# A Linformer attention and MLP-mixer kernel: fixed program order with the next batch's front in steps, crossbar turns of q and u, packed k and v projections

## The chip, the core and the metric

One Trainium2 chip, one of its cores. TensorE multiplies matrices into PSUM (8 banks of 128 x 512 f32), VectorE and ScalarE read PSUM and write SBUF, GpSimd issues the loads that convert f32 to bf16, SyncE issues stores and crossbar turns (transposes made by the DMA engines on the way from SBUF to SBUF). The metric is the device time of one launch in microseconds (us); smaller is better. Profiles are of one execution; their span is about 1.8 us shorter than the time of that launch.

Ratios below are the mean time of one kernel's fast runs over that of the kernel before in the same rounds, so they are not quite the ratio of the medians that stand beside them.

## The reference, cut to what matters

Eight batches; 8 heads of 64; 1024 positions; k and v are projected from 1024 positions to 64 before the attention.

```python
k_proj = np.einsum('ks,bhsd->bhkd', E, k)          # E, F: 64 x 1024
v_proj = np.einsum('ks,bhsd->bhkd', F, v)
scores = q @ k_proj.T / 8;  attn = softmax(scores) # 1024 x 64 per head
x = (attn @ v_proj), heads side by side            # 1024 x 512 per batch
h = relu(x.T @ w_tok1) @ w_tok2                    # token mixing, 256 wide
u = x + h.T
out = u + relu(u @ w_ch1) @ w_ch2                  # channel mixing, 1536 wide
```

I call channel mixing the *main* part (192 matmuls of 512 columns per batch) and everything up to u the *front*.

## The kernel before

The order on each engine is left to a scheduler; `attention(b + 1)` stands before `mixer(b)` in the program. All PSUM tiles come from one pool of 8 banks. The parts that matter:

```python
def attention(b):
    # loads of k, v, q: 8 heads x 128 KB each, on GpSimd
    # q regrouped by head pairs, then turned on TensorE, 32 transposes per batch:
    for hp in range(HP):
        for sj in range(2):
            for ss in range(4):
                nc.tensor.transpose(qt_ps[...], q2_sb[:, hp, si]..., ident)
            nc.vector.tensor_copy(out=qT_sb[...], in_=qt_ps)
    for si in range(NSI):      # v projection: 8 matmuls onto 64 partitions
        nc.tensor.matmul(vproj_ps, FT_sb[:, si, :], v_sb[:, :, si, :], ...)
    ...                        # k projection the same, 8 more
    ...                        # per head pair: two score matmuls on 64 x 64 tiles, exp
    for ss in range(4):        # denominators by a matmul of their own
        nc.tensor.matmul(dn_ps[:, 2*ss : 2*ss+2], lhs, bd_ones, ...)
        nc.tensor.matmul(ou_ps[:, ss, :], lhs, vbd_sb[:, hp, :], ...)
def mixer(b, x_sb):
    ...                        # token mixing, 16 + 16 matmuls of 512 columns
    nc.tensor.transpose(ut_ps[...], u_sb[...], ident)      # 32 per batch
    ...                        # main: gT_ps (up), ReLU, g_ps (down), add u, store
xs[0] = attention(0)
# load wt1, wt2, wc1, wc2 (the last two 1.5 MB each) on the same queue
for b in range(B):
    if b + 1 < B: xs[b + 1] = attention(b + 1)
    mixer(b, xs[b])
```

The softmax here doesn't subtract the row's maximum and nothing guards it: scores larger than these inputs give would overflow.

## Time and profile before

572.56 us median of 4 runs (571.37 to 573.18). TensorE's spacing of two matmuls of 512 columns is 0.217 us, so the main part takes 41.7 us per batch.

| | us |
|---|---|
| first up matmul of batch 0 | 85.0 |
| from the up matmuls of batch 3 (279.31) to those of batch 4 (344.06) | 64.75 |
| of that, main part | 41.7 |
| of that, front | 23 |

The profile's page in 40 slices of the span: busy tenths of TensorE and the load of the DMA engines, then the chain of work that ended last, by engine.

```profile
PE   1540889999999999998999999999999999999997
...
DMA  9999992129502390028601391020001200020012
...
PE 71%; DVE 14%; DMA 6%; POOL 5%; issue 2%; ACT 1%; DVEq 0%; ACTq 0%; POOLq 0%
```

From the seventh slice to the last but one TensorE is busy for at least eight tenths of each slice (nine tenths of nearly all), and it holds 71% of the chain: it is the limit. In the first four slices (57 us) it is busy about half the time at most, while the DMA row is full for the first six.

TensorE's waits, longest in total first (in total, times, longest), and the two ends of the long one in its timeline (start, duration, instruction, in brackets the idle time just before):

```profile
PE qt_ps L109 <- ACT q_sb L99: 34.4, 5, 19.9
PE tp_ps L143 <- DVE kproj_sb L139: 8.0, 8, 1.1
```

```profile
20.81 3.65 PE L109 MATMUL qt_ps<-ident,q_sb 128*128 128x128 bf16 x32 [13.81 <-ACT q_sb L99]
...
56.05 1.03 PE L109 MATMUL qt_ps<-ident,q_sb 128*128 128x128 bf16 x8 [19.88 <-ACT q_sb L99]
...
85.04 5.15 PE L233 MATMUL gT_ps<-uT_sb,wc_sb 128*128 128x512 bf16 x22
```

Batch 1's q transposes waited 19.9 us for loads that stand behind the two large weight loads in the queue; they began at 56.05, and batch 0's main part came after all of batch 1's attention, at 85.04.

The front of one batch in the steady state, on TensorE (starts and durations of merged groups):

```profile
300.27 20.88 PE L242 MATMUL g_ps<-wc_sb,gT_sb 128*128 128x512 bf16 x96
320.99 1.95 PE L109 MATMUL qt_ps<-ident,q_sb 128*128 128x128 bf16 x32
322.87 1.91 PE L120 MATMUL vproj_ps<-v_sb,FT_sb 128*64 128x512 bf16 x8
324.62 1.89 PE L134 MATMUL kproj_ps<-k_sb,ET_sb 128*64 128x512 bf16 x8
327.49 0.29 PE L143 MATMUL tp_ps<-ident,kproj_sb 64*128 64x64 bf16 x4 [0.98 <-DVE kproj_sb L139]
...
333.99 3.61 PE L198 MATMUL h_ps<-x_sb,wt_sb 128*128 128x512 bf16 x16
...
344.06 21.12 PE L233 MATMUL gT_ps<-uT_sb,wc_sb 128*128 128x512 bf16 x96
```

Between the end of the main part (321) and the next (344.06) TensorE spends 2 us on q transposes, 3.6 on the two projections, waits 0.98 for the copy of k, spends 6 us on scores, denominators and outputs (lines left out), and the last 10 (from 333.99) on token mixing, 7, and the u transposes, 3.2 with their waits.

### The profile page before, as it was taken

The page shows a single profiled execution, that of the slowest core. Times are in us where ns is not written, and L with a number is a line of the kernel's source. Part 1 is how long each engine was busy: PE and PEld are TensorE (multiplying, and loading weights), DVE is VectorE, ACT ScalarE, POOL GpSimd, SP SyncE. Part 2 cuts the span into 40 slices and gives each one's busy share as a digit, 9 for nine tenths or more (in the row PEclk, how much of TensorE's full clock was granted, in tenths as well). Part 3 has the DMA queues.
Part 4 walks back from the last instruction along what each step waited for, and adds up shares of the span by engine and source line. Part 5 has one row for each costly group of instructions (what it writes and reads, how often), then busy time and mean ns, then how long its engine had stood idle before and what let it go on. Part 6 is the DMA issues. An engine that isn't in the chain of part 4 may idle for free.

```text
span 570.8 us, 7698 instructions
## 1 busy us (share of the span) xinstructions
PE 509.8 (89%) x3120; PEld 259.4 (45%) x3120; DVE 210.4 (37%) x524; ACT 175.9 (31%) x288; POOL 110.9 (19%) x212
## 2 busy tenths in 40 slices
PE   1540889999999999998999999999999999999997
PEld 0330454454544454445544454445544454445443
DVE  1440571137502572028602563027601563025012
ACT  0221336305260235304260235404261034500720
POOL 8608871006200360006200260000000000000000
PEclk9975889999999999999999999999999999999999
DMA  9999992129502390028601391020001200020012
GB/s 135 208 208 202 201 201 44 38 92 151 91 0 79 102 186 4 27 103 134 109 1 73 94 185 19 20 102 28 1 1 69 80 2 0 18 94 38 1 55 92
DMA packets 39555, 46.90 MB, mean 82 GB/s; under 512 B 4192, under 2 KB 30304, under 8 KB 39520
## 3 DMA queue, kind: packets, MB, share of 16 engines
q0 software_dynamic: 30304, 29.63, 32.4%
q1 hardware_dynamic: 9216, 16.78, 7.5%
q8 instruction: 24, 0.39, 0.3%
q14 instruction: 11, 0.09, 0.1%
HBM read 59.24 MB, written 16.78 MB: 133 GB/s over the span
## 4 chain that ended last, share of the span: by engine, by line
PE 71%; DVE 14%; DMA 6%; POOL 5%; issue 2%; ACT 1%; DVEq 0%; ACTq 0%; POOLq 0%
PE gT_ps L233 29%; PE g_ps L242 29%; DVE u_sb L213 6%; PE h_ps L198 5%; DMA wc_sb<-in_moe_w_ch_dram 4%; DVE qT_sb L114 2%; PE ou_ps L178 2%; PE ut_ps L219 2%; POOL v_sb L90 2%; POOL q_sb L94 2%; PE u_ps L209 2%; POOL k_sb L89 1%; DVE x_sb L183 1%; PE dn_ps L175 1%; DVE vbd_sb L128 1%
## 5 line engine op out<-in xcount | busy, mean ns | idle before, releaser
L233 PE MATMUL gT_ps<-uT_sb,wc_sb 128*128 128x512 bf16 x768 | 169.0, 379 | 0.0
L242 PE MATMUL g_ps<-wc_sb,gT_sb 128*128 128x512 bf16 x768 | 167.1, 379 | 0.0
L238 ACT ACTIVATE gT_sb<-gT_ps 128x512 bf16<-128x512 f32 x184 | 109.0, 597 | 111.6 <-PE gT_ps L233 110.5
L247 DVE TENSOR_TENSOR o_sb<-g_ps,u_sb 128x512 f32<-128x512 f32 x64 | 44.3, 692 | 267.7 <-PE g_ps L242 267.7
L242 PEld LDWEIGHTS <-gT_sb 128*128 128x128 bf16 x768 | 75.1, 98 | 90.7
L233 PEld LDWEIGHTS <-wc_sb 128*128 128x128 bf16 x768 | 74.8, 98 | 90.7 <-issue 3.8
L90 POOL DMA_DIRECT2D v_sb<-in_v_dram x64 | 34.7, 545 | 203.2 <-PE vproj_ps L120 188.5
L99 ACT COPY q_sb<-q_sb 128x1024 bf16<-128x1024 bf16 x23 | 23.1, 1044 | 133.8 <-PE qt_ps L109 109.8
L166 ACT ACTIVATE attnT_sb<-sco_ps 128x512 bf16<-128x512 f32 x64 | 33.0, 602 | 61.2 <-PE sco_ps L161 61.2
L109 PE MATMUL qt_ps<-ident,q_sb 128*128 128x128 bf16 x256 | 19.5, 242 | 34.4 <-ACT q_sb L99 34.4
L213 DVE TENSOR_TENSOR u_sb<-u_ps,x_sb 128x512 bf16<-128x512 f32 x64 | 39.0, 683 | 21.2 <-PE u_ps L209 21.2
L183 DVE TENSOR_TENSOR x_sb<-ou_ps,rdn 128x512 bf16<-128x512 f32 x64 | 41.7, 681 | 1.7
L89 POOL DMA_DIRECT2D k_sb<-in_k_dram x64 | 34.6, 554 | 14.9 <-DMA wc_sb<-in_moe_w_ch_dram 6.8
L94 POOL DMA_DIRECT2D q_sb<-in_q_dram x64 | 34.0, 534 | 10.1 <-issue 5.3
L109 PEld LDWEIGHTS <-q_sb 128*128 128x128 bf16 x256 | 17.6, 109 | 37.1 <-ACT q_sb L99 35.5
L114 DVE COPY qT_sb<-qt_ps 128x512 bf16<-128x512 bf16 x64 | 23.0, 417 | 19.2 <-PE qt_ps L109 19.1
L175 PE MATMUL dn_ps<-bd_ones,attnT_sb 128*128 128x2 bf16 x256 | 27.4, 171 | 2.8 <-ACT attnT_sb L166 1.5
L178 PE MATMUL ou_ps<-vbd_sb,attnT_sb 128*128 128x128 bf16 x256 | 29.8, 221 | 0.0
L198 PE MATMUL h_ps<-x_sb,wt_sb 128*128 128x512 bf16 x128 | 29.7, 386 | 0.0
L209 PE MATMUL u_ps<-hT_sb,wt_sb 128*128 128x512 bf16 x128 | 28.9, 379 | 0.0
L175 PEld LDWEIGHTS <-attnT_sb 128*128 128x128 bf16 x256 | 20.0, 96 | 16.2 <-ACT attnT_sb L166 10.8
L219 PE MATMUL ut_ps<-ident,u_sb 128*128 128x128 bf16 x256 | 21.5, 221 | 5.1 <-DVE u_sb L213 4.6
(46 smaller groups left out, 260.0 us busy)
## 6 DMA issues: line engine op xcount, KB each, us to landing
out_dram<-o_sb SPq DMA_DIRECT2D x64, 256.0 KB, 2.0
k_sb<-in_k_dram POOLq DMA_DIRECT2D x64, 128.0 KB, 4.9
v_sb<-in_v_dram POOLq DMA_DIRECT2D x64, 128.0 KB, 4.9
q_sb<-in_q_dram POOLq DMA_DIRECT2D x64, 128.0 KB, 4.9
wc_sb<-in_moe_w_ch_dram POOLq DMA_DIRECT2D x2, 1536.0 KB, 18.8
wt_sb<-in_moe_w_tok_dram POOLq DMA_DIRECT2D x2, 512.0 KB, 7.4
E_sb<-in_E_dram POOLq DMA_DIRECT2D x1, 128.0 KB, 3.1
F_sb<-in_F_dram POOLq DMA_DIRECT2D x1, 128.0 KB, 3.4
```

The source lines that it names most:

```text
L90: nc.gpsimd.dma_start(out=v_sb[:, h, :, :], in_=v[b, h].rearrange(rr, p=P))
L94: nc.gpsimd.dma_start(out=q_sb[:, h, :, :], in_=q[b, h].rearrange("(p si) d -> p si d", p=P))
L175: nc.tensor.matmul(dn_ps[:, 2 * ss : 2 * ss + 2], lhs, bd_ones, start=True, stop=True)
L178: nc.tensor.matmul(ou_ps[:, ss, :], lhs, vbd_sb[:, hp, :], start=True, stop=True)
L183: nc.vector.tensor_tensor(out=x_sb[:, sj * 4 : sj * 4 + 4, h0 * D : (h0 + 2) * D] .rearrange("p s (j d) -> p s j d", j=2), in0=ou_ps.rearr ...
L198: nc.tensor.matmul(h_ps, wt1_sb[:, sc, tc_i * P : (tc_i + 1) * P], x_sb[:, sc, :], start=(sc == 0), stop=(sc == SC - 1),)
L209: nc.tensor.matmul(u_ps, wt2_sb[:, tc_i, sc::NSI], hT_sb[:, tc_i, :], start=(tc_i == 0), stop=(tc_i == TC - 1),)
L213: nc.vector.tensor_add(out=u_sb[:, sc, :], in0=u_ps, in1=x_sb[:, sc, :])
L233: nc.tensor.matmul(gT_ps, wc1_sb[:, dc, cc * P : (cc + 1) * P], uT_sb[:, dc, s_lo : s_lo + S2], start=(dc == 0), stop=(dc == DMC - 1),)
L238: nc.any.tensor_relu(out=gT_sb[:, cc, s_lo : s_lo + S2], in_=gT_ps)
L242: nc.tensor.matmul(g2_ps, gT_sb[:, cc, sc * P : (sc + 1) * P], wc2_sb[:, cc, :], start=(cc == 0), stop=(cc == CC - 1),)
L247: nc.vector.tensor_add(out=o_sb, in0=g2_ps, in1=u_sb[:, sc, :])
```

## The change

Its intent: take off TensorE what others can do, and let no chain of small dependent steps of the front stop it.

1. The order on every engine is the program's (manual schedule). The front of batch b+1 is a generator of 31 steps, spread as if they were 33; after each block of 4 main matmuls of batch b, zero to two steps are issued.
2. q and u are turned through the crossbar by SyncE's DMAs (batches 1 to 7).
3. The k projection goes to partitions 0 to 63 of a bank and the v projection to 64 to 127, so the two matmuls of a pair use different column tiles of TensorE.
4. The denominator is a 65th column of v (a column of ones), so its matmuls go.
5. Batch 0 is loaded and computed by head pairs; the large weights are loaded last.
6. Main PSUM has 4 banks, the front 2, the output tile 2; 3 of 8 ReLUs go to VectorE.

The diff, cut to its core:

```diff
+    ctx.enter_context(tc.manual_schedule())
+    def turn_q(b):
+        for j in range(2):
+            nc.sync.dma_start_transpose(out=st["qT", b][:, hs]..., in_=st["q", b][:, hs]...)
+    def kv_mm(b, kv_ps, hs, sis):
+        for si in sis:
+            nc.tensor.matmul(kv_ps[0:KP, 0:n], EFT[:, si, 0:KP], st["k", b][:, hs, ds], **f)
+            nc.tensor.matmul(kv_ps[KP:P, 0:n], EFT[:, si, KP:P], st["v", b][:, hs, ds], **f)
-                    nc.tensor.matmul(
-                        dn_ps[:, 2 * ss : 2 * ss + 2], lhs, bd_ones, start=True, stop=True
-                    )
+            nc.tensor.matmul(                       # ou_step, 130 columns, 4 per head
+                ou[:, s // 2, o : o + 2 * D1], at[:, s * P : (s + 1) * P], vbd[:, h, :], ...)
+    def front(b):
+        turn_q(b)
+        yield
+        for j in range(4):
+            kv_mm(b, kv_ps, slice(0, H), range(2 * j, 2 * j + 2))
+            if j < 3:
+                yield
+        kv_vec(b, kv_ps, kprojs, slice(0, H))       # 1 ScalarE copy, 3 VectorE copies
+        if b + 1 < B:
+            load_kv(b + 1, (0, H)); load_q(b + 1, (0, H))
+        yield
+        kt_step(...)                                # k turned on TensorE
+        yield
+        ats = {0: score_step(b, 0, kT, front_ps)}
+        yield
+        for h in range(H):
+            if h + 1 < H:
+                ats[h + 1] = score_step(b, h + 1, kT, front_ps)
+            ou_step(b, h, ats.pop(h))
+            yield
+        ...                                         # token mixing, 8 + 8 steps
+            if s % 2 == 1:
+                nc.sync.dma_start_transpose(out=st["uT", b][:, s - 1 : s + 1]..., ...)
+    front_first()                                   # batch 0 by head pairs
+    for b in range(B):
+        for n, _ in enumerate(mains()):             # one block of 4 main matmuls
+            want = 0 if n < first else min(n_front, 1 + (n - first) * n_front // (last - first))
+            while done < want:
+                done += 1
+                next(fr, None)
```

`front_first` computes `attn(0)`, then `attn(hp)` and `mix(hp - 1)` in turn, then `mix(3)`.

## The prediction

> **What bounds the kernel now.** TensorE. The page gives matmuls 89% of the 570.8 us span and the chain of waits puts 71% on it. The timeline shows two regimes. (a) Start: the first channel-mixing (up) matmul begins at 85.0 us. Until then TensorE waits 34.4 us in total for the regrouped q (waits view); the DMA strip reads full for 80 us, and the two weight DMAs of 1536 KB stand in front of batch 1's loads. (b) Steady state: one batch takes 64.7 us (300.27 to 365.01). Channel mixing is 192 matmuls of 512 columns at 0.217 us = 41.7 us. The other 23 us are the front: q transposes 1.9, v and k projections 3.6, a hole of about 1.7 around the k transposes, scores 1.75, denominator/output pairs 3.75, token mixing 6.9, u transposes 3.2 with waits.
>
> **What the change does per batch, on TensorE.**
> - q and u transposes leave TensorE from batch 1 on: -5.1 us.
> - k and v projections as two 64-column tiles side by side: 16 slots become 8. Traced score pairs took 0.215 us: -1.8 us.
> - The denominator column goes into the output product (130 columns): 32 pairs become 32 matmuls of about 0.06 us (q transposes' pitch): about -1.9.
> - The holes of the front are filled by channel mixing: about -1.7.
> - Added: about 26 changes of tiling mode. The Trainium skill, "TensorEngine Tiling (Array Packing)", Key Properties, says a mode change drains the array; the trace's outputs-to-scores step costs 0.15 instead of 0.06 us, so about 0.1 each, +2.6.
> - Added waits: the output tile has one buffer, and reciprocal 0.19 plus multiply 0.68 on VectorE, queued behind ReLUs of 0.69, must finish in about 1.4 us between steps: estimate +1.5. Last u turn before the next batch's up matmuls: +0.5.
>
> Front about 16 us, so a period near 58 instead of 64.7, all on the critical path: about 7 x 6.7 = 47 us.
>
> **Start.** Batch 0 is loaded by head pairs, small weights early, large ones behind, and computed pair by pair. By the traced 0.2 MB/us, pair 1 lands near 15 us; attention plus mixing of one pair is an estimated 10.5 us chain, much of it waits. Channel mixing of batch 0 begins near 52 (46 to 58) instead of 85. But the old start had batch 1's attention done too, so only about half of the 33 us is net.
>
> **Sum.** 52 + 7 x 58 + 41.7 (last batch, no front) + 3.7 (tail as now) = 503; I say 502 us, 8 times in 10 between 485 and 525. Faster by over 2%: 95%; within 2%: 4%; slower: 1%.
>
> **Signs in the profile.** First up matmul near 52 us; batches 57 to 59 us apart; no q or u transposes on TensorE after about 55 us; k and v matmuls starting in pairs within some 10 ns; matmul busy share above 93% after the start; a few us of waits of output matmuls for the x multiply; crossbar transposes landing within 9 us (q) and 5 us (last u) of issue.
>
> **What would make it wrong.** The crossbar. The skill, "Advanced Engine Details and Errata", X-Bar Transpose, says transposes are as fast as regular DMAs (350-400 GB/s); no run here shows it yet. At a quarter of that, q (1 MB) needs over 10 us and the u turns queue up: TensorE, whose order is now fixed, stalls 3 to 5 us per batch and the total is near 530. If mode changes cost nothing and VectorE is never late, 485. A start near 60 adds 8.

## The result and the profile after

513.45 us median of 4 runs (509.96 to 513.99), against 572.56: ratio 0.896 (95% interval 0.893 to 0.899). The prediction was 502, range 485 to 525.

The same rows of the page:

```profile
PE   2576999999999999999999999999999999999996
...
DMA  9998959375954569167863669157772550052012
...
PE 84%; DVE 7%; ACT 3%; DMA 2%; issue 1%; POOL 1%; ACTq 0%; POOLq 0%
```

TensorE is at nine tenths from the fifth slice (51 us) to the last but one and holds 84% of the chain.

The start of the main part, and the steady state of one batch in TensorE's timeline:

```profile
30.59 0.31 PE L159 MATMUL kv_ps<-k_sb,EFT 128*64 128x128 bf16 x1
...
30.70 0.31 PE L159 MATMUL kv_ps<-k_sb,EFT 128*64 128x128 bf16 x1
...
55.97 12.28 PE L368 MATMUL g_ps<-uT,wc 128*128 128x512 bf16 x56
```

```profile
292.17 5.34 PE L368 MATMUL g_ps<-uT,wc 128*128 128x512 bf16 x24
297.45 0.40 PE L159 MATMUL kv_ps<-k_sb,EFT 128*64 128x512 bf16 x1
297.45 0.40 PE L160 MATMUL kv_ps<-v_sb,EFT 128*64 128x512 bf16 x1
297.69 0.38 PE L159 MATMUL kv_ps<-k_sb,EFT 128*64 128x512 bf16 x1
...
298.00 1.04 PE L368 MATMUL g_ps<-uT,wc 128*128 128x512 bf16 x4
...
303.95 0.41 PE L165 MATMUL kt_ps<-ident,kprojs 64*128 64x64 bf16 x8 [0.34 <-DVE kprojs L150]
...
306.43 0.40 PE L179 MATMUL sco<-qT,kT 64*64 64x512 bf16 x2 [0.25 <-DVE kT L170]
...
307.74 0.40 PE L179 MATMUL sco<-qT,kT 64*64 64x512 bf16 x2
308.07 0.40 PE L192 MATMUL ou_ps<-vbd,attnT 128*128 128x130 bf16 x4
...
350.39 1.89 PE L368 MATMUL g_ps<-uT,wc 128*128 128x512 bf16 x8
```

The first up matmul starts at 55.97 instead of 85.04. From 292.17 to 350.39 a batch takes 58.22 us instead of 64.75. The projections of k (L159) and v (L160) start together. There are no q or u transposes in this stretch, and only short waits.

As a check, the stretches add up to the spans. Before, 85.0 + 41.7 (main of batch 0) + 6 x 64.7 + 10 (mixing of batch 7; its attention was done earlier) + 41.7 + 3.7 (tail) = 570 (570.8). After, 56.0 + 61.5 (first period) + 5 x 58.2 + 57.9 + 41.7 + 3.7 = 512 (512.2). The start gives 29 us, but before it also held batch 1's attention, which the steady state of the new kernel has to do: some 13 us of TensorE's time (q 1.9, projections 3.6, hole 1.7, scores 1.75, outputs 3.75). So about 16 us come from the start and about 42 from seven periods that are 6 us shorter.

### The profile page after: what moved, and what is told of

Its sections match the earlier page's. It is cut to its first block, busy times and chain, and to the rows that moved or that the text cites. A ratio compares the mean times of both kernels' runs of the same rounds, so it can differ in the third digit from the quotient of the medians.

```text
span 512.2 us, 6273 instructions
## 1 busy us (share of the span) xinstructions
PE 475.9 (93%) x2561; PEld 219.3 (43%) x2584; DVE 215.6 (42%) x384; ACT 129.5 (25%) x227; POOL 33.7 (7%) x47
## 3 DMA queue, kind: packets, MB, share of 16 engines
q1 hardware_dynamic: 68064, 31.99, 25.6%
HBM read 59.24 MB, written 16.78 MB: 148 GB/s over the span
## 4 chain that ended last, share of the span: by engine, by line
PE 84%; DVE 7%; ACT 3%; DMA 2%; issue 1%; POOL 1%; ACTq 0%; POOLq 0%
PE d_ps L390 32%; PE g_ps L368 30%; PE u_ps L255 5%; PE h_ps L243 5%; PE sco L179 4%; PE ou_ps L192 4%; PE kv_ps L159 3%; DMA q_sb<-in_q_dram 2%; DVE x_sb L199 2%; DVE g L375 2%; PE h_ps L300 1%; DVE u_sb L313 1%; PE u_ps L309 1%; DVE kprojs L150 1%; ACT kprojs L149 1%
## 5 line engine op out<-in xcount | busy, mean ns | idle before, releaser
L368 PE MATMUL g_ps<-uT,wc 128*128 128x512 bf16 x768 | 186.0, 381 | 0.3
L390 PE MATMUL d_ps<-wc,g 128*128 128x512 bf16 x751 | 181.3, 379 | 0.5
L377 ACT ACTIVATE g<-g_ps 128x512 bf16<-128x512 f32 x120 | 71.7, 597 | 253.3 <-PE g_ps L368 253.3
L390 PEld LDWEIGHTS <-g 128*128 128x128 bf16 x768 | 75.1, 98 | 87.3
L368 PEld LDWEIGHTS <-wc 128*128 128x128 bf16 x768 | 69.7, 98 | 82.3 <-issue 14.1
L397 DVE TENSOR_TENSOR o_sb<-d_ps,u_sb 128x512 f32<-128x512 f32 x64 | 44.3, 692 | 102.6 <-PE d_ps L390 102.6
L375 DVE TENSOR_SCALAR g<-g_ps 128x512 bf16<-128x512 f32 x72 | 49.8, 692 | 69.7 <-PE g_ps L368 69.4
L184 ACT ACTIVATE attnT<-sco 128x512 bf16<-128x512 f32 x64 | 37.6, 594 | 16.9 <-PE sco L179 16.3
L255 PE MATMUL u_ps<-R_sb,wt 128*128 128x512 bf16 x112 | 33.3, 379 | 0.4
L243 PE MATMUL h_ps<-x_sb,wt 128*128 128x512 bf16 x106 | 31.8, 379 | 1.2 <-DVE x_sb L199 1.1
L159 PE MATMUL kv_ps<-k_sb,EFT 128*64 128x512 bf16 (+1 forms) x88 | 21.3, 354 | 1.2 <-DVE EFT L136 0.8
L160 PE MATMUL kv_ps<-v_sb,EFT 128*64 128x512 bf16 (+1 forms) x88 | 21.1, 354 | 1.0 <-DMA v_sb<-in_v_dram 1.0
## 6 DMA issues: line engine op xcount, KB each, us to landing
v_sb<-in_v_dram POOLq DMA_DIRECT2D x4, 256.0 KB, 11.1
```

The source lines that it names most:

```text
L184: nc.scalar.activation(out=at, in_=sco, func=ACT.Exp, scale=scale)
L243: nc.tensor.matmul(h_ps, wt1[:, s, t * P : (t + 1) * P], st["x", b][:, s, :], start=(s == 0), stop=(s == SC - 1),)
L255: nc.tensor.matmul(u_ps, wt2[:, t, s::SC], st["R", b][:, t, :], start=(t == 0), stop=(t == TC - 1),)
L368: nc.tensor.matmul(g_ps, wc1[:, dc, cc * P : (cc + 1) * P], uT[:, 4 * sh : 4 * sh + 4, dc, :], start=(dc == 0), stop=(dc == DMC - 1),)
L375: nc.vector.tensor_relu(out=o, in_=g_ps)
L377: nc.scalar.activation(out=o, in_=g_ps, func=ACT.Relu)
```

## The experiments

Theory A: TensorE is the limit, so each part is worth the TensorE time that it takes off, and interleaving makes the waits of the front free. The rivals are in the expectations. All kernels gave correct results; each was compared with the kernel before in the same rounds (its median was 571.4 to 571.9 us there). A *period* is the time from one batch's first up matmul to the next's, read from the timeline of the profiled run, as a mean over the five periods between batches 1 and 6 (steady). In the profiled runs the first up matmul came at 53.0 to 56.0 us in all kernels that leave the code of batch 0 as it is in the changed kernel (e1 to e5 and e9), so smaller differences of the start say nothing. Two parts of the change have no run of their own: the fixed order without steps (item 1), and the split of PSUM and ReLUs (item 6).

| run | median us | ratio to before | first up matmul | first period | steady period |
|---|---|---|---|---|---|
| before | 572.56 | 1 | 85.0 | 64.6 | 64.77 |
| changed kernel | 513.45 | 0.896 | 56.0 | 61.5 | 58.22 |
| e1 u turns on TensorE | 530.14 | 0.929 | 53.0 | 64.0 | 60.87 |
| e2 q turns on TensorE | 529.63 | 0.926 | 54.1 | 61.8 | 60.88 |
| e3 k, v not packed | 521.37 | 0.912 | 55.2 | 61.3 | 59.58 |
| e4 fewer mode changes | 510.35 | 0.893 | 55.5 | 59.0 | 58.19 |
| e5 front in one piece | 645.92 | 1.130 | 56.0 | 74.6 | 78.4 |
| e6 before, other load order | 557.63 | 0.975 | 68.7 | 66.0 | 65.0 |
| e7 start overlapped | 499.91 | 0.875 | 44.3 | 60.0 | 58.23 |
| e8 idle matmuls at the start | 511.46 | 0.895 | 54.8 | 61.5 | 58.23 |
| e9 fewer mode changes, casts moved | 509.42 | 0.890 | 56.0 | 58.8 | 57.98 |
| e10 denominators apart | 518.33 | 0.908 | 54.6 | 60.8 | 59.08 |
| e11 e7 and e9 together | 511.94 | 0.894 | 45.0 | 72.6 | 57.98 |
| e12 e7, fewer mode changes, spaced | 492.5 in 2 runs, 502.7 in 4 | see there | 44.7 | 59.4 | 56.93 |

### e1 and e2: one turn back on TensorE

```diff
-            if s % 2 == 1:
-                nc.sync.dma_start_transpose(out=st["uT", b]..., in_=st["u", b]...)
+            if s % 2 == 0 and s > 0:
+                turn_u(b, s - 2)        # 8 transposes, one ScalarE copy
             yield
+        turn_u(b, SC - 2)
+        yield
-        n_front = 33
+        n_front = 34                    # e2: the same for q in 4 steps, n_front 36
```

> Only the u turns of batches 1 to 7 go back to TensorE (32 transposes and 4 ScalarE copies per batch), still in steps between the blocks. Theory A (the interleaving hides the crossbar, so what counts is TensorE's time): 7 x 32 x 0.058 us = +13 us, about 526 us, period 60.6. Rival B (the crossbar turns cost something by landing late or crowding the other transfers): less than +6, or faster than the changed kernel.

> Only the q turns of batches 1 to 7 go back to TensorE. Theory A: +13 us, about 526. Rival B (q's crossbar turn delays the scores or the loads): below +6.

Each costs about 16.5 us over the changed kernel, 2.65 us per period. 32 transposes at 0.058 us explain 1.9. Most of the rest is in the steady waits of e1's timeline:

```profile
313.86 0.40 PE L179 MATMUL sco<-qT,kT 64*64 64x512 bf16 x2 [1.11 <-DVE kT L170]
```

In the changed kernel the scores waited 0.25 us for the copy of the turned k (306.43 above); here 1.11. One more step in the front shifted the steps against the blocks, so that one block instead of two lies between the k turn and the scores. The crossbar is thus worth 2 x 1.9 us per batch of TensorE time, as theory A says; B is refuted. The other 0.8 us per period is a matter of step positions.

### e3: k and v on the same partitions

```diff
-            nc.tensor.matmul(kv_ps[KP:P, 0:n], EFT[:, si, KP:P], st["v", b][:, hs, ds], **f)
+            nc.tensor.matmul(v_ps[0:KP, 0 : H * D], EFT[:, si, KP:P], st["v", b][:, :, ds], **f)
```

> k and v projections of batches 1 to 7 written to the same 64 partitions of two banks, so that the two matmuls of a pair cannot run side by side; everything else as changed. Theory A: 8 more slots of 0.215 us per batch, minus nothing: +12 us, about 525, the pair's starts 0.215 us apart instead of under 0.01. Rival C (the packed pair is bound by its weight loads or by the mode changes, so packing saves little): below +5.

```profile
300.96 0.38 PE L167 MATMUL kv_ps<-k_sb,EFT 128*64 128x512 bf16 x1
301.18 0.38 PE L168 MATMUL v_ps<-v_sb,EFT 128*64 128x512 bf16 x1
```

The matmuls now start 0.215 us apart, and the period grows by 1.36 us, the total by 8. That is less than 8 x 0.215 = 1.7, because the waits around the turn of k (0.34 and 0.25 us per batch) fell to 0.13 and 0.10 us behind the longer steps. Packing is worth its TensorE time; rival C is refuted.

### e10: denominators apart

```diff
+            for c in (slice(D, D1), slice(0, D)):      # 2 columns, then 128
                 nc.tensor.matmul(ou[...][:, :, c], at[:, s * P : (s + 1) * P], vbd[...][:, :, c], ...)
```

> The changed kernel with the denominator columns as matmuls of their own again (2 columns, then 128, into the same output tile), 32 more matmuls per batch. Theory A: in the trace of before a pair took 0.082 us and here a merged matmul takes 0.058, so 32 x 0.025 = +0.8 us per batch, if the waits stay, +6 us, about 519. What the prediction said (a matmul of 0.06 us saved each, -1.9 us per batch): +13, about 526.

The period grows by 0.86 us and the total by 5. The small matmul costs 0.027 us beside the large one with the same weights, not the 0.06 us that the prediction gave it.

### e5: the front in one piece

```diff
-            want = 0 if n < first else min(n_front, 1 + (n - first) * n_front // (last - first))
+            want = 0 if n < first else 1          # the other 30 steps after the main part
```

> The front of the next batch runs in one piece between two batches' channel mixing, instead of in steps between its blocks (the q turn stays early). Theory A (the front is a chain of small waits: multiply after output 1.5 us per head, k transposes, ReLU of the token mixing, the last u turn of some 4.5 us, that only interleaving hides): about 30 us per front instead of 17, +90 us, near 605, slower than the kernel before. Rival E (the gain is the work taken off TensorE; interleaving is a detail): 515 to 535.

TensorE's largest waits in e5, then three rows of its timeline, then the engines in two stretches (window, its length, busy time and count of TensorE, weight loads, VectorE, ScalarE and GpSimd, granted clock, DMA share, GB/s):

```profile
PE ou_ps L192 <- DVE x_sb L199: 35.7, 53, 1.1
PE g_ps L368 <- DMA uT<-u_sb: 21.9, 14, 2.2
```

```profile
335.24 0.40 PE L165 MATMUL kt_ps<-ident,kprojs 64*128 64x64 bf16 x8 [1.32 <-DVE kprojs L150]
337.13 0.83 PE L179 MATMUL sco<-qT,kT 64*64 64x512 bf16 x4 [1.48 <-DVE kT L170]
...
365.57 1.04 PE L368 MATMUL g_ps<-uT,wc 128*128 128x512 bf16 x4 [1.33 <-DMA uT<-u_sb]
```

```profile
334.00:338.00 4.00, 1.23 (x12) 0.42 (x12) 2.38 (x4) 0.95 (x2) 2.63 (x3) 0.93 0.58 81
340.00:346.00 6.00, 4.32 (x24) 1.90 (x24) 2.90 (x7) 1.96 (x4) 0.00 (x0) 0.50 1.24 207
```

The same instructions take 78.4 us per batch instead of 58.2, 13% slower than the kernel before. TensorE waits 35.7 us in all for the multiply of the head before (some 0.55 at most heads), 1.3 and 1.5 us around the k turn, and 3.1 us per batch for the last u turns. With the waits the clock falls: after 334 to 338, where TensorE works 1.2 of 4 us, it reads 0.50, and 16 matmuls of token mixing take 6.6 us (3.6 in the kernel before). The same instructions run at the full clock in the changed kernel's steady periods, so the placing brings it; what in the waits sets it off is not shown. My 605 had the waits but not the clock. Rival E is refuted: without the interleaving, everything else in the change loses to the kernel before.

### e6: the old kernel with the weights loaded later

```diff
     xs[0] = attention(0)
     ...                       # wt1, wt2
+    xs[1] = attention(1)
     ...                       # wc1, wc2, 1.5 MB each
```

> The kernel before, with one thing changed: the two 1.5 MB channel-mixing weights are loaded after batch 1's q, k, v instead of before them. Theory F (half of the change's gain is the start, and most of that was the place of the weights in the load queue): first up matmul near 62 us instead of 85, about 550 us. Rival G (the start gain comes from computing batch 0 by head pairs): under 5 us gained.

The first up matmul moves from 85.0 to 68.7 and the time falls by 14 us, ratio 0.975: less than the 22 expected (batch 1's q transposes now begin at 41.5 us, but batch 1's attention still comes before batch 0's main part), more than G allowed. So about a quarter of the whole gain was to be had by moving one line.

### e7 and e8: what bounds the new start

e7 makes `attn` and `mix` generators that yield at their waits and runs `attn(hp)` and `mix(hp - 1)` in alternating steps; e8 only adds idle matmuls.

```diff
-        for hp in range(1, HP):
-            attn(hp)
-            mix(hp - 1)
+        for hp in range(1, HP):                         # e7
+            parts = [attn(hp), mix(hp - 1)]
+            while parts:
+                for p in list(parts):
+                    if next(p, "end") == "end":
+                        parts.remove(p)
+    for _ in range(16):                                 # e8
+        nc.tensor.matmul(warm_ps, warm_sb[:, 0:P], warm_sb, start=True, stop=True)
```

> The changed kernel with attention of head pair n and token mixing of pair n-1 of batch 0 in alternating steps. Theory H (from 20 us on the start is bound by a chain of waits, 11.7 us per pair, not by the loads): pairs of 8 us, first up matmul near 46 us instead of 56, -10 us, about 503. Rival I (the loads bound it): within 2 us of 513.

> The changed kernel with 16 idle matmuls of 512 columns on constant data in the first 8 us. Matmuls of 128 columns start 0.106 us apart from 9 to 41 us, and 0.055 us apart after, although the granted clock reads 1.00. Theory J (TensorE is at half rate for lack of work before, and once at full rate stays there): spacing 0.055 us from the start, pairs shorter by 3 us, -6 us or more. Rival K (the gaps of about 1 us in each pair bring it back to half rate within some us): under 2 us gained.

e7 starts batch 0's main part at 44.3 instead of 56.0 and takes 499.9 us, 13.5 less than the changed kernel. The q transposes of pairs 2 and 3 (128 columns, 8 of them):

```profile
19.12 1.03 PE L283 MATMUL qt_ps<-ident,q_sb 128*128 128x128 bf16 x8 [0.26 <-DMA q_sb<-in_q_dram]
...
31.05 1.03 PE L283 MATMUL qt_ps<-ident,q_sb 128*128 128x128 bf16 x8
```

```profile
26.07 0.62 PE L283 MATMUL qt_ps<-ident,q_sb 128*128 128x128 bf16 x8
...
32.53 0.62 PE L283 MATMUL qt_ps<-ident,q_sb 128*128 128x128 bf16 x8
```

In the changed kernel a pair takes 11.9 us (19.12 to 31.05); in e7 6.5 (26.07 to 32.53), and the transposes run at the full rate (0.62 instead of 1.03 us). e8 shows that warming alone does not do it (windows as in e5):

```profile
12.00:16.00 4.00, 1.56 (x14) 0.82 (x12) 1.57 (x5) 1.99 (x3) 1.43 (x2) 0.89 1.16 206
16.00:18.00 2.00, 0.92 (x14) 0.75 (x14) 0.90 (x2) 0.00 (x0) 0.96 (x2) 0.50 1.23 203
```

The idle matmuls do bring the full rate (the eight transposes of E and F at 9 us take 0.66 us instead of 1.07), but at 16 us the clock is at half again, after 4 us in which TensorE was busy 1.56 us, with no single wait above 1.12 us. The 2 us by which e8's median is lower lie within the spread of the runs (509.8 to 512.9 against 510.0 to 514.0), as K expected. Rival I falls: the loads do not set the 11.9 us. Theory H is only half of it. In the changed kernel's pair TensorE is idle for 2.8 of 11.9 us and works 9.15, mostly at the half rate; in e7's it works 5.50 for the same 78 matmuls and is idle for 1.0. Overlapping filled the waits and the full rate came with it; since e8 did not hold the rate, what each gives by itself stays open.

It is tempting to say that the share of busy time sets the clock. Two stretches of 3.41 us, the first of the changed kernel, the second of e4, show that this is not enough:

```profile
74.15:77.56 3.41, 1.95 (x16) 0.77 (x16) 2.88 (x5) 0.60 (x1) 2.14 (x3) 1.00 0.50 53
```

```profile
70.63:74.04 3.41, 1.95 (x17) 0.76 (x18) 2.70 (x5) 0.73 (x2) 1.95 (x3) 1.00 0.69 82
```

TensorE works 1.95 us in both, and the longest wait is 1.11 us in both. In the next 3.41 us the clock reads 0.50 in the changed kernel and 1.00 in e4.

### e4 and e9: fewer changes of tiling mode

```diff
-        for j in range(4):
-            kv_mm(b, kv_ps, slice(0, H), range(2 * j, 2 * j + 2))
-            if j < 3:
-                yield
+        kv_mm(b, kv_ps, slice(0, H), range(SC))
...
-            if h + 1 < H:
-                ats[h + 1] = score_step(b, h + 1, kT, front_ps)
+            if h % 2 == 0 and h + 2 < H:
+                for hh in (h + 2, h + 3):
+                    ats[hh] = score_step(b, hh, kT, front_ps)
```

e9 adds a new order of the copies behind the projections: one cast of v, the copy of k, and the other cast on ScalarE.

> Same matmuls, fewer changes of tiling mode: k and v projections in one step instead of four, scores of two heads in one step, 12 mode changes per batch instead of 26. Theory A (each change costs 0.1 us, read from the trace): 7 x 14 x 0.1 = -10 us, about 503.5. Rival D (the 0.1 us is only how the matmul ends are modelled): no difference, 513.

> The run with fewer mode changes gained only in its first period; its later periods were 58.2 us, as in the changed kernel, because the scores now wait 1.11 us per batch for the copy of the transposed k, which stands on VectorE behind two casts of v (0.69 us each) and a ReLU. Here one of those casts goes ahead of the copy of projected k (while ScalarE makes it) and the other goes to ScalarE. Theory A (mode changes do cost 0.1 us each, and the wait ate the gain): that wait falls to 0.4 us or less, period 57.2 to 57.5, about 504. Rival D (mode changes cost nothing real): period stays at 58.2, about 510.

Neither moved the steady period much (58.19 and 57.98 against 58.22). The waits of one batch:

```profile
300.06 0.62 PE L179 MATMUL sco<-qT,kT 64*64 64x512 bf16 x4 [1.11 <-DVE kT L170]
```

```profile
298.21 0.39 PE L170 MATMUL kt_ps<-ident,kprojs 64*128 64x64 bf16 x8 [1.34 <-DVE kprojs L156]
...
299.50 0.62 PE L184 MATMUL sco<-qT,kT 64*64 64x512 bf16 x4
```

In e4 the wait for the turned k rose from 0.25 to 1.11 us. In e9 that went, but the turn itself waits 1.34 us for the copy of k. I had moved the wait, not removed it. The sum fits theory A: TensorE's waits in one steady period add up to 1.0 us in the changed kernel, 2.2 in e4 and 2.1 in e9, so 1.2 to 1.3 us per batch were gained elsewhere. But both runs missed the expected time; e12 shows the gain without the waits.

### e11 and e12: both improvements together

e11 is e7 with e9. e12 is e7 with e4, with the casts as in the changed kernel, and with empty steps:

```diff
         turn_q(b)
         yield
+        yield
+        yield
         kv_mm(...); kv_vec(...)
-        if b + 1 < B: load_kv(b + 1, (0, H)); load_q(b + 1, (0, H))
+        yield
         yield
         kt_step(...)
         yield
+        yield
+        if b + 1 < B: load_kv(b + 1, (0, H)); load_q(b + 1, (0, H))
         ats = {h: score_step(b, h, kT, front_ps) for h in range(2)}
```

> The overlapped start (e7), fewer mode changes and the moved casts together. If they add: 499.9 minus 7 x 0.8 us, minus some 2 us in the first period: about 492.

> e11 lost in its first period (72.6 us) because the loads of the batch after were issued at 59.4 us, while the q turn was in flight (13.1 us to landing instead of 4.7), and later because the k transposes waited 1.34 us. Here the overlapped start and the 12 mode changes stay, the casts are as in the changed kernel, empty steps give the chain from the projections to the scores two more blocks, and the next loads are issued only at the scores. If that reading holds: q turn 5 us again, first period under 60 us, waits for the transposed k under 0.3 us, later periods about 57.0, total about 491. If the collision with the loads was not the cause, the first period stays above 65.

e11 took 511.9 us, not 492. Its first period is 72.6 us (a row of TensorE's timeline, then the two q turns of batch 1):

```profile
65.64 1.06 PE L184 MATMUL sco<-qT,kT 64*64 64x512 bf16 x4 [2.86 <-DMA qT<-q_sb]
```

```profile
DMA to landing us min/median/max: 7.4/13.1/18.8
```

e12's q turns of batch 1, a row of its first period, and its steady front:

```profile
DMA to landing us min/median/max: 4.6/7.5/10.5
```

```profile
70.30 0.62 PE L179 MATMUL sco<-qT,kT 64*64 64x512 bf16 x4 [1.07 <-DMA qT<-q_sb]
...
286.39 0.40 PE L165 MATMUL kt_ps<-ident,kprojs 64*128 64x64 bf16 x8
...
288.55 0.62 PE L179 MATMUL sco<-qT,kT 64*64 64x512 bf16 x4
```

In e11 the two q turns of batch 1 took 7.4 and 18.8 us to land (4.6 at the median in the changed kernel), beside batch 2's loads of k and v, which GpSimd issued from 59.4 us on because the projections were done sooner; the scores waited 2.9 and 6.6 us for them. In e12's steady periods the k transposes and the scores no longer wait, and the period is 56.93 us, 1.29 less than in the changed kernel for 14 mode changes fewer. The output matmuls now wait 0.16 us at some heads, so TensorE's waits add up to 0.9 us per period, nearly as in the changed kernel (1.0), and some 0.09 us is left for each change. Rival D is refuted.

One part of e12 did not do what I wrote. The loads stand at the scores in the program, but the profile has them at 60.8 us: GpSimd waits for data only (here for the last projection, which frees k's tile), not for TensorE's place in the program. The first q turn landed in 4.6 us; the second met the loads, took 10.5 us, and scores waited 1.07 us for it. So the reading that loads beside the turns cost e11 its first period fits both runs, but no run kept them apart.

And e12 has two times on a single core: 492.0 and 493.1 us, and 502.6 to 503.1 in four of six runs, with a granted clock of 0.985 to 0.988 instead of 0.996 and 0.997. The profiled run is one of the fast ones; no profile of a slow one exists, so what makes them slow stays open. e7, with one time in all four runs (499.2 to 500.8), is the best that is settled; e12's fast runs were 7 us below it, its slow runs 3 us above.

## Why the prediction was right, point by point

- *TensorE bounds it; the gain is in the front and the start.* Right: e1, e2, e3 and e10 each lose about the TensorE time that they put back.
- *Crossbar -5.1 us per batch.* Of the right kind; 3.7 of it is transposes (2 x 32 x 0.058); the rest goes with the waits around the u transposes, of which the profile marks 0.6 us as idle (0.37 and 0.20). The risk named, a slow crossbar stalling TensorE, did not come: at its own place in the program no q or u turn was waited for in the steady state. (e5 and e11 show that it can be, when little else lies between or loads run beside it.)
- *Packing -1.8.* Measured 1.4 with its effect on waits (e3).
- *Denominators -1.9.* Mis-sized: 0.86 (e10).
- *Mode changes +2.6.* Right: 26 of about 0.1. They can be read in the timeline: from the second pair of k and v (297.69) to the next up matmul (298.00) it is 0.31 us, where a plain step is 0.215; and e12 took 14 away for 1.3 us, with nearly the same waits.
- *Output waits +1.5, last u turn +0.5.* Mis-sized: in the period above the output matmuls wait 0.25 us and the first token mixing 0.16, both at the last head; the u turn 0.
- *Period 58.* Measured 58.22, with some luck: the errors above cancel, and the prediction's own terms add up to a front of 17.1 us, a period of 58.8, where it wrote 16 and 58.
- *Start 52, a pair 10.5 us.* Measured 56.0 and 11.9 (the next pair 11.1). One step that failed: I took the trace's full-rate durations for the start. Matmuls of 128 columns start 0.11 us apart there (30.59 to 30.70 above), and 0.055 later. Another: pair 1's v and q, expected near 15 us, came at 17.8 and 19.1, and TensorE waited for both (1.02 and 0.26 us). The same start took 53.0 to 56.0 us in the other profiles.
- *Signs.* Most of the others came: after the start TensorE is busy for 97% of the span (442.5 of 456 us), a q turn lands within 5.4 us and a u turn within 4.4, and the last transposes of q or u on TensorE begin at 55.7 us.
- *First period like the others.* It is 3.3 us longer: a wait of 1.11 us for the turned k before 77.2 us, four up matmuls behind it at half rate (1.87 us instead of 1.04), and a wait of 0.78 for an exponential at 86.5 us.

The sum misses by 4 us in the start and 5 in the periods, and the span is 1.8 us below the time, which the sum had left out.

## What to carry to other kernels

When one engine is the limit, a chain of small dependent steps costs little if it is issued in small steps between that engine's long blocks (1.0 us of waits per batch here), and a great deal if it runs in one piece: in e5 TensorE's clock also fell to half (same instructions, 26% more time than the changed kernel). What a step costs is then decided by how many blocks lie between it and what it needs, so when steps are added, removed or merged, read those waits again: e1, e4 and e9 each lost about 1 us per batch that way. Before restructuring a start, look at the order of the loads and at what could run in TensorE's waits: one moved line gave 14 us in the old kernel, and overlapping two chains gave 13.5 in the new one.

## What the Trainium skill lacked or had wrong

- "TensorEngine Tiling (Array Packing)", Key Properties, says that a change of tiling mode drains TensorE, without a figure. Here a change after or before matmuls of 512 columns cost 0.09 to 0.1 us (14 fewer per batch: 58.22 to 56.93 us, e12).
- "Advanced Engine Details and Errata", X-Bar Transpose, says that transposes are as fast as regular DMAs, 350 to 400 GB/s. Here each of q's two turns (512 KB) landed 4.6 us after issue and a u turn (256 KB) 3.1, a plain store of 256 KB 2.1; batch 1's two q turns, issued at 62.46 us, had both landed at 69.32, 1.05 MB in 6.9 us or 153 GB/s with the latency in it. From the queues' shares an estimate, rough because packets of one engine overlap (the DMA share reads up to 1.31): hardware DMAs moved 31.99 MB in 25.6% of 512 us on 16 engines after, and 16.78 MB (the stores) in 7.5% of 571 us before, so 15.2 MB (14.7 of it turns, the rest E and F) took about 88 us, 170 GB/s; the stores 390 GB/s. "DMA: Bandwidth & Descriptors", Rules for kernel authors, says that a transpose next to ordinary DMAs needs nothing; that is so for correctness here, but beside loads of 2 MB (k and v) the two q turns took 7.4 and 18.8 us (e11).
- "TensorE: Matmul & The Clock Gate", Part 1 and "HAM oscillation", gives idle gaps above some 3.4 us as what brings the half clock; its section on a second failure mode lets frequent short idles do it too, without a measure. In e8 it came with no wait above 1.12 us, after 4 us with TensorE busy 1.56 us; in e5 after 4 us with 1.23. Which short waits do it stays open: after 3.41 us with TensorE busy 1.95 us and a longest wait of 1.11 the clock fell in the changed kernel (74.15 to 77.56) and did not in e4 (70.63 to 74.04).
- No page that I read says what the granted clock shows before its first record: in the changed kernel it reads 1.00 from 9 to 41 us, where matmuls of 128 columns start 0.11 us apart, as they do in e8 where it reads 0.50 (17.5 to 18.2 us), and half that far apart once the rate is full.
